# Two modes of the last weight unit loaded by SP in fp32 and cast by GpSimd, and another pace for the last jobs

## The chip, the cores and the metric

The kernel runs on one core of a Trainium2 chip. The metric is device time in microseconds of one launch. The kernel before takes 435.25 us, the median of three runs (435.19 to 435.46).

## What is computed

A causal attention with a window of 64 positions over q, k, v of 8 batches, 8 heads, 576 positions and 64 channels, and behind it a spectral mixing layer over the model width of 512:

```python
rel = pos[:, None] - pos[None, :]
mask = (rel >= 0) & (rel < 64)
attn = softmax(where(mask, q @ k.T / 8, -1e9))
x = (attn @ v)                     # laid out as (8, 576, 512)

X = np.fft.rfft(x, axis=1)         # the first 64 modes are kept
Xr, Xi = X[:, :64].real, X[:, :64].imag
Yr = einsum('bmd,mde->bme', Xr, w_r) - einsum('bmd,mde->bme', Xi, w_i)
Yi = einsum('bmd,mde->bme', Xr, w_i) + einsum('bmd,mde->bme', Xi, w_r)
y = np.fft.irfft(Y, n=576, axis=1)
u = x + y
out = u + np.maximum(u @ w_ch, 0.0)
```

w_r and w_i are 64 matrices of 512 x 512 in fp32 each, 134 MB in all, and every one is read once. The output is 9.4 MB of fp32.

## The kernel before

**Weights.** A mode is one of the 64 matrices. Four modes make a group; a group is taken in two halves hb of 256 input rows, and each half in two parts ri: 0 from w_r, 1 from w_i. One such piece, four modes of 256 rows, is a unit: 2 MB of fp32 in memory, 1 MB of bf16 in SBUF. `steps` is the order of (group, half), `wlist` the list of loads made from it, with `parts` the transfers that a load is cut into: one for the four modes in general, and for the very last load, `(len(steps) - 1, 1)`, three, of two modes, one and one.

`load_weights` issues loads on GpSimd's DMA queue (line 165), which turns fp32 into bf16 on the way. A load needs a tile of a ring. In the last phase there are only the NRA = 3 tiles of `ringA`, so a load is issued when TensorE has done its matmuls with the load three before it. `wtiles` says where a mode lies; `mode_half` (line 188) runs the matmuls of a unit. For the last unit of all it sorts them by mode, so that mode p comes first, then p + 1, p + 2, p + 3.

**Phases.** Under the loads run, one after the other: the attention; the transforms of its output; then, from the step `i == EARLY` on, the products x @ w_ch of all tiles and, under the last eight units, the jobs that bring back and multiply the modes that are complete by then. At `i == EARLY` some pools are closed (`ringB` among them) and others opened: `utpool`, from which the first output tile `utx` of [128, 2, 512] fp32 is later taken, and copies of trig tables by SP's queue (lines 951 and 952).

**Jobs.** `jobs` is a list of pairs (prepare, done). `advance` prepares the next job and finishes the one before it. When the group NGRP - 1 is complete, with eight units to go, 36 jobs are put in: eight `batch_job`s (four transposes, then four matmuls with w_ch) and, for the first four batches, seven small ones each: `early_u` (inverse transform of a tile or two) and `add_late` (one matmul, line 703, and an addition on VectorE, line 704). After each unit the loop advances until `given` has reached `want`, which grows by 36 / 6 a unit. Before the last unit but one all jobs left are finished (`half == n0 + n1 - 2`).

**The end.** After the last unit (lines 627 to 656) the last two groups are turned, multiplied and added by `early`, `full_u`, `full_z` and `last`, which write the output tile by tile, most of it from SP's queue (line 821). Output tiles come from `new_ut`: first `utx`, then the three tiles of `ringA`, two homes in each, taken round.

**Order.** The scheduling is by hand: each engine and each DMA queue runs its instructions in the order in which the program writes them; waits are added where data or memory ask for it.

Of the kernel before, what the change touches and what calls it, by code (L numbers as in the profile page):

```python
# [9 lines left out]
FP32 = mybir.dt.float32  # L10
# [16 lines left out]
def kernel(  # L27
# [10 lines left out]
    nc = tc.nc  # L38
    B, H, S, D = q.shape
    NM = moe_w_r.shape[0]  # L40
    DM = moe_w_ch.shape[0]
# [7 lines left out]
    HALF = DM // 2  # L49
    NJ = 2  # L50
# [5 lines left out]
    def pool(name, bufs=1, **kw):  # L56
        opened.append(tc.alloc_tile_pool(name=name, bufs=bufs, **kw))
        return opened[-1]

    def close(*pools):  # L60
        for x in pools:
            opened.remove(x)
            x.release()

    NLB = 4
# [33 lines left out]
    steps = [(grp, 0) for grp in range(EARLY)] + [(grp, 1) for grp in range(EARLY)]  # L99
# [4 lines left out]
    wlist = []  # L104
    for at, (grp, hb) in enumerate(steps):
        for ri in range(2):
            p = 4 * grp
            if (at, ri) == ONES:
                parts = [[(p, p + 1)], [(p + 2,)], [(p + 3,)]]
            elif (at, ri) == (len(steps) - 1, 1):  # L110
                parts = [[(p, p + 1), (p + 2,), (p + 3,)]]
            else:
                parts = [[(p, p + 1, p + 2, p + 3)]]
            wlist += [(at, part, hb, ri) for part in parts]
# [15 lines left out]
        lent.update((wstart[at] + i, t) for i, t in enumerate(of))  # L130
    lentY = Yall.rearrange("p (g j) e -> p g j e", j=NJ)
    NLY = 1
    wtiles, spent = {}, set()
    held = {"a": [], "b": [], "y": []}
    room = {"a": NRA, "b": NRB, "y": NLY}
    nload = 0
# [5 lines left out]
    def load_weights(n):  # L142
        nonlocal nload
        while nload < len(wlist):
            at, parts, hb, ri = wlist[nload]
            if 2 * n <= sum(len(ps) for ps in parts):
                return
            if nload in lent:
                w = lent[nload]
            else:  # L150
                open_to = "a" if at >= 2 * EARLY else "aby" if at < EARLY + 2 else "ab"
                h = min(open_to, key=lambda h: held[h][0] if len(held[h]) == room[h] else -1)
                if len(held[h]) == room[h]:
                    if held[h][0] not in spent:
                        return
                    held[h].pop(0)
                held[h].append(nload)
                if h == "y":
                    w = lentY
                else:  # L160
                    w = {"a": ringA, "b": ringB}[h].tile([128, 4, NJ, DM], BF16, name="wi" if ri else "wr", tag="wt")
            src = moe_w_i if ri else moe_w_r
            to = 0
            for ps in parts:
                nc.gpsimd.dma_start(  # L165
                    out=w[:, to:to + len(ps)],
                    in_=src[ps[0]:ps[-1] + 1, HALF * hb:HALF * hb + HALF, :].rearrange("g (p j) e -> p g j e", j=NJ))
                for i, p in enumerate(ps):
                    wtiles[p, hb, ri] = w[:, to + i]
                to += len(ps)  # L170
            nload += 1
            n -= to

# [21 lines left out]
    with tc.manual_schedule():  # L197
# [175 lines left out]
        at = scratch[:, 3 * NTF * NM:3 * NTF * NM + NTF]  # L373
# [104 lines left out]
        for it in range(-3, NU + 3):  # L478
# [23 lines left out]
            g = starts.get(it + 2)  # L502
# [3 lines left out]
            g = starts.get(it + 1)  # L506
# [35 lines left out]
        def bank(h, shape=(128, DM), dtype=FP32, name=None):  # L542
            return banks[h].tile(list(shape), dtype, name=name or "ps" + h, tag="bank")
# [69 lines left out]
        def advance():  # L613
            if jobs:
                prepare, done = jobs.pop(0)
                pend.append((prepare(), done))
                if len(pend) < 2:
                    return
            if pend:
                tr, done = pend.pop(0)  # L620
                done(tr)
# [108 lines left out]
        def early_jobs(b):  # L730
            early_u(b, (1,))
            add_late(b, 0)
            early_u(b, (3,))
            add_late(b, 1)
            add_late(b, 2)
            early_u(b, (0, 2))
            add_late(b, 3)
# [7 lines left out]
        NT = len(tiles)  # L745
# [6 lines left out]
        def x_jobs(pl, lo, hi):  # L752
            for i in range(lo, hi):
                def done(tr, i=i):
                    XW[i] = pl.tile([128, DM], FP32R, name=f"xw{i}")
                    nc.vector.tensor_copy(out=XW[i], in_=multiply(tr))  # L756
                jobs.append((lambda i=i: transposed(tiles[i][0]), done))
# [13 lines left out]
        ps, pu = {}, {}  # L771
# [11 lines left out]
        def tail_xw(n, js=(0, 1)):  # L783
            for i in [seq[n][j] for j in js]:
                ps[i] = bank("zt"[n % 2 == 0])
                nc.tensor.matmul(out=ps[i], lhsT=ident_r, rhs=XW[i], start=True, stop=True)  # L786
# [81 lines left out]
                nc.tensor.matmul(out=ps[i], lhsT=trigIr[:, at:at + 128], rhs=zrows(b), start=False, stop=True,  # L868
                                 skip_group_check=True)

        uts, homes = {}, []
        utpool, taken_uts = None, 0
        NUT = 2 * NRA + 1

        def new_ut():
            nonlocal taken_uts
            if not homes:
                homes.append(utpool.tile([128, 2, DM], FP32, name="utx"))
            elif taken_uts == len(homes) < NUT:
                t = ringA.tile([128, 4, DM], FP32, name="ut", tag="wt")  # L880
                homes.extend([t[:, 0:2], t[:, 2:4]])
            taken_uts += 1
            return homes[(taken_uts - 1) % NUT]
# [47 lines left out]
        NX0 = 10  # L931
        x_jobs(pool("xp0", reuse_waits="tile"), 0, NX0)
        psm = None
        half = given = 0
        n0, n1 = 2 * EARLY, 4 * (NGRP - EARLY)
        for i, (grp, hb) in enumerate(steps[EARLY:]):
            f, l = grp < EARLY or hb == 0, hb == 1
            if i == EARLY:
                while tables:
                    tables.pop(0)()  # L940
                while jobs or pend:
                    advance()
                close(stmp2, yp, ringB)
                Zall = pool("zall", side="right").tile([2 * NM, B, DM], FP32R, name="Zall")
                x_jobs(pool("xp1", side="right", reuse_waits="tile"), NX0, NT)
                utpool = pool("utpool", side="right", reuse_waits="tile")
                nc.vector.memset(YT[:, :, :, rows], 0.0)
                nc.vector.tensor_scalar(out=trz.rearrange("p c g k -> p c (g k)"), scalar1=0.0, scalar2=None, op0=ALU.mult,
                                        in0=ident.unsqueeze(1).to_broadcast([128, NDCH, 128]))
                for g in range(4):  # L950
                    nc.sync.dma_start(out=trigL[32 * g:32 * g + 16], in_=trigI[rows, 0:512])
                    nc.sync.dma_start(out=trigLr.bitcast(FP32)[32 * g:32 * g + 16], in_=trigIr.bitcast(FP32)[rows, 0:512])
                given = 0
            if f:
                psm = [bank("m"), bank("m")] if grp == LAST + 1 else bank("m")
            for ri in range(2):
                if half == n0 + n1 - 2:
                    while jobs or pend:
                        advance()
                if half == n0 + n1 - 1:  # L960
                    late["first"] = bank("z")
                    late[0][1]()
                    tail_xw(0)
                mode_half(psm, grp, hb, ri, f, l)
                load_weights(len(wlist))
                while ready:
                    ready.pop(0)()
                for t in tables[0:2]:
                    t()
                del tables[0:2]  # L970
                if half == 0:
                    nc.gpsimd.dma_start(out=wch, in_=moe_w_ch.rearrange("(c p) e -> p c e", p=128))
                if l and ri:
                    finish_group(grp, psm)
                    if grp == NGRP - 1:
                        ready.pop(0)()
                        for b in range(B):
                            batch_job(b)
                            if 0 < b <= NLB:
                                early_jobs(b - 1)  # L980
                half += 1
                if half <= n0:
                    want = max(half - 4, 0) * NX0 // (n0 - 4)
                elif half <= n0 + n1 - 8:
                    want = (half - n0) * (NT - NX0) // (n1 - 8)
                else:
                    want = NT - NX0 + (half - n0 - n1 + 8) * (B + 7 * NLB) // 6
                while given < want:
                    advance()
                    given += 1  # L990
# [74 lines left out]
```

## Time and profile before

| | |
|---|---|
| runs, median | 435.25 us |
| profiled execution, its own time | 434.85 us |
| its span, first to last instruction | 433.1 us |
| TensorE matmul, busy | 322.2 us |
| VectorE, busy | 230.0 us |
| ScalarE, busy | 179.9 us |
| GpSimd, busy | 101.3 us |
| DMA, moved | 93.64 MB, 216 GB/s over the span |
| read from HBM | 163.58 MB |
| last unit's matmuls | 395.82 to 397.01 us |

The span is what the profile sees between the first and the last instruction; 1.75 us of the execution lie around it. Bytes moved are counted as written, so a weight counts two bytes there and four in what is read from HBM. The DMA share is that of sixteen engines together; it can pass 1, since packets overlap. In a timeline each row has its start, its length, the engine, the line of the kernel, the operation, what it writes and reads, and in brackets the idle time before it with what ended it. A row of the windows has, after the stretch, its length and the busy time of TensorE's matmuls, its weight loads, VectorE, ScalarE and GpSimd with the number of instructions, then the granted clock, the DMA share and GB/s.

### The profile page before, as it was taken

How to read it: one execution, taken by the hardware profiler on the slowest of the kernel's cores; microseconds unless marked ns; L12 is line 12 of the kernel's file. 1: busy time of each engine (PE TensorE's matmuls, PEld its weight loads, DVE VectorE, ACT ScalarE, POOL GpSimd, SP SyncE). 2: the span in 40 equal slices, each digit the busy share in tenths (PEclk: the TensorE clock that was granted, in tenths of full speed). 3: DMA queues.
4: the chain of work that ended last, by engine and by line, in shares of the span. 5: the costliest groups of instructions: out<-in, count | busy, mean ns of one | idle time of the engine just before them, and what ended most of it. 6: DMA issues, size and time to landing. Idle time of an engine off the chain costs nothing.

```text
span 433.1 us, 10990 instructions
## 1 busy us (share of the span) xinstructions
PE 322.2 (74%) x4758; PEld 216.0 (50%) x4802; DVE 230.0 (53%) x472; ACT 179.9 (42%) x322; POOL 101.3 (23%) x150
## 2 busy tenths in 40 slices
PE   6888899898999999962207353767564768789994
PEld 3666667576677677641104221444343445345652
DVE  8588787876776777863104111222131315653994
ACT  5665757666666666520201100122121213325842
POOL 8322222222131231131102100012111111110990
PEclk9999999999999999996557756588899889989998
DMA  8999999999999999999999999999999999993798
GB/s 210 211 211 212 211 212 212 210 211 212 212 213 210 211 212 212 212 212 212 211 259 213 217 212 212 212 212 212 212 212 212 212 211 211 212 211 72 243 367 295
DMA packets 47280, 93.64 MB, mean 216 GB/s; under 512 B 2688, under 2 KB 3136, under 8 KB 47232
## 3 DMA queue, kind: packets, MB, share of 16 engines
q0 software_dynamic: 41008, 81.73, 99.7%
q1 hardware_dynamic: 5328, 9.77, 6.6%
q10 hardware_dynamic: 896, 1.44, 0.9%
q8 instruction: 37, 0.61, 0.5%
q14 instruction: 11, 0.09, 0.1%
HBM read 163.58 MB, written 9.44 MB: 400 GB/s over the span
## 4 chain that ended last, share of the span: by engine, by line
DMA 50%; PE 36%; issue 6%; ACT 3%; DVE 2%; POOL 1%; DVEq 0%; POOLq 0%
DMA wi<-in_moe_w_i_dram 29%; DMA wr<-in_moe_w_r_dram 22%; PE tr L231 6%; PE s L278 4%; PE s L290 3%; PE pt L298 3%; PE psm L188 3%; PE vb L243 3%; PE o L318 2%; PE s L270 2%; PE pst L786 1%; PE psz L786 1%; PE psz L610 1%; PE pst L868 1%; PE px L341 1%
## 5 line engine op out<-in xcount | busy, mean ns | idle before, releaser
L610 PE MATMUL psz<-wch,tr 128*128 128x512 f32 x176 | 62.5, 488 | 11.3 <-DMA wch<-in_moe_w_ch_dram 11.0
L756 DVE CAST xw<-psz 128x512 fp32r<-128x512 f32 x36 | 24.9, 692 | 86.1 <-PE psz L610 86.1
L584 ACT CAST tr<-ptx 128x512 fp32r<-128x512 bf16 x36 | 21.1, 586 | 102.9 <-PE ptx L603 102.9
L282 DVE TENSOR_REDUCE mx<-s 128x4 fp32r<-128x512 f32 x72 | 49.5, 688 | 26.9 <-PE s L278 26.4
L188 PEld LDWEIGHTS <-XQ 128*32 128x32 bf16 x448 | 18.9, 174 | 78.3 <-issue 53.8
L165 POOL DMA_DIRECT2D wi<-in_moe_w_i_dram x32 | 23.4, 732 | 103.6 <-PE psm L188 70.2
L188 PE MATMUL psm<-wi,XQ 128*32 128x512 bf16 x208 | 19.8, 454 | 37.1 <-DMA wi<-in_moe_w_i_dram 37.1
L610 PEld LDWEIGHTS psz<-wch,tr 128*128 128x128 f32 x176 | 37.4, 235 | 18.4 <-issue 11.6
L292 ACT ACTIVATE p<-s 128x512 bf16<-128x512 f32 x72 | 39.7, 604 | 12.8 <-PE s L290 12.8
L165 POOL DMA_DIRECT2D wr<-in_moe_w_r_dram x27 | 20.3, 754 | 95.8 <-PE psm L188 77.8
L188 PE MATMUL psm<-wr,XQ 128*32 128x512 bf16 x184 | 18.6, 483 | 28.1 <-DMA wr<-in_moe_w_r_dram 27.2
L278 PE MATMUL s<-kT,qT 64*64 64x128 bf16 (+1 forms) x576 | 29.2, 222 | 6.7 <-issue 6.7
L235 ACT COPY kT<-tr 128x576 bf16<-128x576 bf16 x32 | 23.2, 724 | 20.2 <-PE tr L231 20.2
L235 ACT COPY qT<-tr 128x576 bf16<-128x576 bf16 x32 | 23.3, 729 | 10.6 <-PE tr L231 10.6
L301 DVE COPY pts<-pt 128x1024 bf16<-128x1024 bf16 (+1 forms) x40 | 25.2, 629 | 4.5 <-PE pt L298 3.1
L278 PEld LDWEIGHTS <-qT 64*64 64x64 bf16 x576 | 17.8, 107 | 17.9 <-issue 17.5
L290 PE MATMUL s<-mx,ident_r 128*128 128x512 f32 x72 | 26.2, 437 | 0.0
L635 DVE TENSOR_TENSOR stg<-psm,Yfour 128x512 bf16<-128x512 f32 x10 | 6.9, 689 | 36.3 <-PE psm L188 36.3
L235 ACT COPY vT<-tr 128x576 bf16<-128x576 bf16 x32 | 23.3, 728 | 4.1 <-PE tr L231 4.0
L298 PE MATMUL pt<-ident_bf,p 128*128 128x128 bf16 x288 | 23.3, 221 | 1.7 <-issue 1.6
L218 POOL DMA_DIRECT2D rawk<-in_k_dram x15 | 8.1, 540 | 66.0 <-PE tr L231 59.9
L330 DVE TENSOR_TENSOR x_sb<-o,r 128x512 bf16<-128x512 f32 x32 | 22.1, 691 | 1.1
(217 smaller groups left out, 598.3 us busy)
## 6 DMA issues: line engine op xcount, KB each, us to landing
wi<-in_moe_w_i_dram POOLq DMA_DIRECT2D x29, 1024.0 KB, 18.7
wr<-in_moe_w_r_dram POOLq DMA_DIRECT2D x27, 1024.0 KB, 17.7
out_dram<-ut SPq DMA_DIRECT2D x23, 256.0 KB, 2.8
rawv<-in_v_dram POOLq DMA_DIRECT2D x16, 288.0 KB, 14.9
rawk<-in_k_dram POOLq DMA_DIRECT2D x15, 288.0 KB, 13.9
rawq<-in_q_dram POOLq DMA_DIRECT2D x15, 288.0 KB, 13.8
x_sb<-in_moe_w_r_dram POOLq DMA_DIRECT2D x2, 1024.0 KB, 15.4
out_dram<-utx SPq DMA_DIRECT2D x5, 256.0 KB, 3.1
```

What stands on the lines that cost most here:

```text
L165: nc.gpsimd.dma_start(out=w[:, to:to + len(ps)], in_=src[ps[0]:ps[-1] + 1, HALF * hb:HALF * hb + HALF, :].rearrange("g (p j) e -> p g j e" ...
L188: nc.tensor.matmul(out=ps[32 * g:32 * g + 32, 0:e], lhsT=of.rearrange("k s b m -> k (s b) m")[:, (3 * j + 1 - ri) * B:(3 * j + 5 - ri) * B ...
L231: nc.tensor.transpose(out=pt[ro, j, :], in_=raw[ro, TH * half + j, :], identity=ident_bf[ro, ro])
L235: nc.scalar.copy(out=to, in_=pt.rearrange("p j n -> p n j"))
L278: nc.tensor.matmul(out=s[ro, t, lo:128], lhsT=lq, rhs=kT[ro, 64 * n - 64 + lo:64 * n + 64], start=False, stop=True, skip_group_check=True)
L282: nc.vector.tensor_reduce(out=mx, in_=s, axis=AX.X, op=ALU.max, negate=True)
L290: nc.tensor.matmul(out=s, lhsT=ident_r, rhs=mx.unsqueeze(2).to_broadcast([128, 4, 128]), start=False, stop=True, skip_group_check=True)
L292: nc.scalar.activation(out=p[:, 4 * c2:4 * c2 + 4, :], in_=s, func=ACT_F.Exp, scale=EX_SCALE)
L298: nc.tensor.transpose(out=pt[:, t, :], in_=st[u]["p"][:, t, :], identity=ident_bf)
L301: nc.vector.tensor_copy(out=ps[:, 0:nt, :], in_=pt[:, 0:nt, :])
L610: nc.tensor.matmul(out=pz, lhsT=tr[:, c, :], rhs=wch[:, c, :], start=(c == 0), stop=(c == NDCH - 1))
L756: nc.vector.tensor_copy(out=XW[i], in_=multiply(tr))
```

## The change

In the last step, mode p of both units is no longer loaded by GpSimd's queue. SP's queue loads it in fp32 into the first output tile, 8 partitions at a time, so 16 transfers of 32 KB for a mode, and GpSimd casts it into its place in the weight tile. There is one such home: the transfers for the second unit are issued behind the cast of the first one. The cast stands in GpSimd's order behind the transfers of the same unit's other modes. The other three modes stay with GpSimd's queue: in one transfer for the unit of w_r, in two (p + 1 and p + 2, then p + 3) for that of w_i. The home `utx` is taken at `i == EARLY` and the first 16 transfers are issued there, ahead of SP's copies of the trig tables. The due count of the last jobs grows by 36 x 2 / 11 a unit in place of 36 / 6.

```diff
             elif (at, ri) == (len(steps) - 1, 1):
-                parts = [[(p, p + 1), (p + 2,), (p + 3,)]]
+                parts = [[(p,), (p + 1, p + 2), (p + 3,)]]
+            elif (at, ri) == (len(steps) - 1, 0):
+                parts = [[(p,), (p + 1, p + 2, p + 3)]]
...
+    BY_SP = list(range(len(wlist) - 2, len(wlist)))
+    homes = []
...
             for ps in parts:
-                nc.gpsimd.dma_start(
-                    out=w[:, to:to + len(ps)],
-                    in_=src[ps[0]:ps[-1] + 1, HALF * hb:HALF * hb + HALF, :].rearrange("g (p j) e -> p g j e", j=NJ))
+                if nload in BY_SP and to == 0:
+                    own = w
+                else:
+                    nc.gpsimd.dma_start(
+                        out=w[:, to:to + len(ps)],
+                        in_=src[ps[0]:ps[-1] + 1, HALF * hb:HALF * hb + HALF, :].rearrange("g (p j) e -> p g j e", j=NJ))
                 for i, p in enumerate(ps):
                     wtiles[p, hb, ri] = w[:, to + i]
                 to += len(ps)
+            if nload in BY_SP:
+                nc.gpsimd.tensor_copy(out=own[:, 0], in_=homes[0])
+                BY_SP.pop(0)
+                if BY_SP:
+                    stage_by_sp()
             nload += 1
             n -= to
+
+    def stage_by_sp():
+        at, parts, hb, ri = wlist[BY_SP[0]]
+        src = (moe_w_i if ri else moe_w_r)[parts[0][0], HALF * hb:HALF * hb + HALF, :].rearrange("(p j) e -> p j e", j=NJ)
+        for p in range(0, 128, 8):
+            nc.sync.dma_start(out=homes[0][p:p + 8], in_=src[p:p + 8])
...
-        uts, homes = {}, []
-        utpool, taken_uts = None, 0
+        uts, taken_uts = {}, 0
...
-            if not homes:
-                homes.append(utpool.tile([128, 2, DM], FP32, name="utx"))
-            elif taken_uts == len(homes) < NUT:
+            if taken_uts == len(homes) < NUT:
...
-                utpool = pool("utpool", side="right", reuse_waits="tile")
+                homes.append(pool("utpool", side="right", reuse_waits="tile").tile([128, 2, DM], FP32, name="utx"))
+                stage_by_sp()
...
-                    want = NT - NX0 + (half - n0 - n1 + 8) * (B + 7 * NLB) // 6
+                    want = NT - NX0 + (half - n0 - n1 + 8) * (B + 7 * NLB) * 2 // 11
```

## The prediction

> **What bounds the kernel now.** First the page: its totals of the engines and of the DMA queues.
>
> ```profile
> PE 322.2 (74%) x4758; PEld 216.0 (50%) x4802; DVE 230.0 (53%) x472; ACT 179.9 (42%) x322; POOL 101.3 (23%) x150
> ...
> q0 software_dynamic: 41008, 81.73, 99.7%
> ...
> q8 instruction: 37, 0.61, 0.5%
> ```
>
> q0, GpSimd's load queue, is busy in 99.7% of the engine time: up to the last weight load the DMA engines set the pace. q8 is TensorE's own code: 4758 + 4802 = 9560 instructions, and 0.61 MB / 9560 is 64 bytes each.
>
> Then the timeline of GpSimd, for the spacing of the loads:
>
> ```profile
> 372.50 0.74 POOL L165 DMA_DIRECT2D wi<-in_moe_w_i_dram  x1 [4.21 <-PE psm L188]
> 377.50 0.74 POOL L165 DMA_DIRECT2D wr<-in_moe_w_r_dram  x1 [4.26 <-PE psm L188]
> 382.46 1.81 POOL L165 DMA_DIRECT2D wi<-in_moe_w_i_dram  x3 [4.22 <-PE psp L648]
> 401.60 2.52 POOL L835 TENSOR_TENSOR utx<-x_sb,utx 128x512 f32<-128x512 f32 x2 [17.33 <-ACT utx L834]
> ```
>
> A unit of four modes every 4.98 us, so one mode is 4.98 / 4 = 1.245 us of all sixteen DMA engines. GpSimd is free between the issues, and from 384.3 to 401.6.
>
> Then one-microsecond windows over the end of the loads (the last two columns are the DMA share and GB/s):
>
> ```profile
> 389.00:390.00 1.00, 0.90 (x5) 0.29 (x3) 1.00 (x3) 0.28 (x1) 0.00 (x0) 1.00 1.11 205
> 390.00:391.00 1.00, 0.64 (x8) 0.49 (x8) 0.60 (x2) 1.00 (x3) 0.00 (x0) 1.00 0.98 182
> 391.00:392.00 1.00, 1.00 (x9) 0.73 (x6) 0.93 (x2) 0.37 (x1) 0.00 (x0) 1.00 0.68 127
> 392.00:393.00 1.00, 1.00 (x9) 0.82 (x8) 0.52 (x2) 0.82 (x2) 0.00 (x0) 1.00 0.62 117
> 393.00:394.00 1.00, 1.00 (x6) 0.65 (x5) 0.00 (x0) 1.00 (x3) 0.00 (x0) 1.00 0.57 107
> 394.00:395.00 1.00, 1.00 (x19) 0.50 (x17) 0.00 (x0) 0.69 (x2) 0.00 (x0) 1.00 0.48 90
> 395.00:396.00 1.00, 1.00 (x11) 0.57 (x11) 0.00 (x0) 0.13 (x1) 0.00 (x0) 1.00 0.19 35
> ```
>
> The share doesn't stop, it halves at about 391 and runs on to 396: about half the engines are done some 5 us ahead of the rest. Taking 1.12 as full, what is missing from 390 to 396 is 0.14 + 0.44 + 0.50 + 0.55 + 0.64 + 0.93 = 3.2, or 3.2 / 1.12 = 2.9 us of all sixteen engines. Evenly dealt, the loads would end near 393.1. The lag has a likely source: q8's 0.5% of 16 engines' span is 0.005 x 16 x 433.1 = 34.6 us of engine time, 4.3 us each if it falls on eight engines.
>
> Last the timeline of TensorE, for when it takes each load:
>
> ```profile
> 371.54 0.66 PE L188 MATMUL psm<-wr,XL 128*32 128x512 bf16 x8 [0.56 <-DMA wr<-in_moe_w_r_dram]
> 376.53 0.66 PE L188 MATMUL psm<-wi,XL 128*32 128x512 bf16 x8 [1.24 <-DMA wi<-in_moe_w_i_dram]
> 381.46 0.68 PE L188 MATMUL psm<-wr,XL 128*32 128x256 bf16 x16 [0.97 <-DMA wr<-in_moe_w_r_dram]
> 387.54 0.67 PE L188 MATMUL psm<-wi,XL 128*32 128x256 bf16 x16
> 388.14 0.88 PE L703 MATMUL psz<-Zall,trigIr 128*128 128x512 f32 x2
> 394.44 0.67 PE L188 MATMUL psm<-wr,XL 128*32 128x256 bf16 x16
> 395.82 1.19 PE L188 MATMUL psm<-wi,XL 128*32 128x256 bf16 x16
> ```
>
> Up to 381.46 it waits for loads; after that for none. The load taken at 394.44 was issued at 377.50 and, with the 13.9 us of its neighbour in the chain of waits, there by 391.4: TensorE is 3.0 us late with its jobs. Then the last unit starts at 395.82 and ends at 397.01, just behind the last landing. Both bound the end: DMA by its late half, TensorE by its jobs. From 397.4 to 426 the chain is TensorE almost without a gap, so the 36 us behind the last unit move with its end.
>
> **The change, part by part.**
>
> *Bytes.* Two modes, 0.5 MB of fp32 each, go from q0 to SP's queue. I take the same engine time per byte read: wch, fp32 into fp32, went through in the page's slice of 259 GB/s, 47 above its neighbours; 47 x 10.8 us is 0.5 MB, just its wider writes, so reading sets the rate. In all nothing is saved; it matters on which engines the SP bytes fall. Eight rows can occupy at most eight engines if a row isn't split, and no view names a packet's engine, so the price has two ends. On the early half: those engines get 2 x 2.49 us and lose 2 x 1.245 us, so they end 2.49 later (391 to 393.5), the late half 2.49 sooner (396.0 to 393.5). On the late half: 396.0 + 2.49 = 398.5. Spread over all: 0. The only rows of narrow traffic are q8's, and they show that it can sit on one half; SP's queue is another one, and the half that already carries q8 is the less likely for it. I take the early half, as a lean and not a reading.
>
> [...]
>
> *First stage.* Its 16 transfers run at about 230 to 245, are cast at 378, and their bytes are already in the sum above. In SP's queue they stand ahead of the eight copies of trigL and trigLr (229.8 to 239.4), which slip some 10 us; their reader comes at 400. Cost 0; the load queue keeps two units waiting, so no engine runs dry.
>
> *First cast.* On GpSimd behind the issue at 377.50. The issue has three modes, not four (0.7). A GpSimd copy of 128x1024 fp32 is not in the trace: above, two adds of 128x512, 2.52 us; below, its memset of 128x1024 bf16, 1.01 us. I take 1.6. Done at 377.5 + 0.7 + 1.6 = 379.8; the next issue is due at 382.46, so nothing queues behind it.
>
> *Second stage.* It starts at 379.9. Two rows of SP's timeline for an issue, and two of the list of DMA issues for a landing (last column, us):
>
> ```profile
> 238.15 0.59 SPq L951 DMA_DIRECT2D trigL<-trigI  x1
> 405.40 10.59 SPq L821 DMA_DIRECT2D out_dram<-ut  x16
> ```
>
> ```profile
> out_dram<-ut SPq DMA_DIRECT2D x23, 256.0 KB, 2.8
> ...
> trigLr<-trigIr SPq DMA_DIRECT2D x4, 32.0 KB, 4.8
> ```
>
> 0.59 to 0.66 us an issue: the sixteenth goes out at 379.9 + 15 x 0.6 = 388.9. It lands 2.8 us (queues empty) to 4.8 us (loads running) later, at 391.7 to 393.7. The second cast ends 1.0 to 2.5 us on: 392.7 to 396.2. By 4.0 and 1.6 I take 394.5. It is the last thing on GpSimd before 401.6, but the whole last unit waits for it, since that unit takes mode p first.
>
> *Jobs.* Due counts after each of the last loads: 6, 12, 18, 24, 30, 36 become 6, 13, 19, 26, 32, 36. The total is the same; the early stretches have 0.56 + 1.24 + 0.97 = 2.77 us of waiting for loads to take them in. The stretch before 394.44 loses two add_late jobs, the 0.88 at 388.14, and the one before it swaps an early_u pair and an add_late for two add_lates, some 0.5 less. Together 1.3 us (0.8 to 1.9): the matmul of 394.44 comes at 393.1.
>
> *Sum.* The last unit starts 395.82 - 394.44 = 1.38 behind that: 394.5 by TensorE, 394.5 by the cast, with the loads down by 393.5. Its 16 matmuls take 1.1: end 395.6 against 397.0, a gain of 1.4 us. Worst within this case, cast at 396.2: end 397.3, a loss of 0.3; best, TensorE 1.9 sooner and the cast no bound: 2.2. The profiled execution took 434.85 (span 433.1), which becomes 433.45; the median of the runs is 0.4 higher, 435.25, and gives 433.85.
>
> **The rivals.**
>
> *Nothing moves* (SP's bytes spread over all engines, or the second cast so late that it eats the gain): the last landing stays at 396.0 or the cast comes there. For it: no view shows engines, and the cast's margin is under 2 us. 434.9 to 435.6.
>
> *Slower by the late half.* SP's eight engines are the ones that already finish at 396. Then the last landing is 398.5, the cast hardly sooner, and the last unit ends near 399.0: +2.0 us, 437.3, up to 438. It decides as soon as more than half of SP's bytes are on late engines. For it: nothing in the trace names the engines. Against: the same as above.
>
> *Slower by narrow transfers.* Each 32 KB goes into eight rows of SBUF; if a transfer needs 1.2 us and not the 0.6 of its issue, the second stage ends at 379.9 + 19 + 2 = 401, the cast at 402.6, and the unit at 403.7: +6.7, 442. It decides from about 0.7 us a transfer (379.9 + 15 x 0.7 + 4.0 + 1.6 = 396.0, where the last unit starts now). Against: the trigL copies into 16 rows came out at their spacing of 0.6 with the loads running.
>
> [...]
>
> **How the numbers follow.** 0.61 for the forecast (433.85, own range 432.9 to 435.0), 0.14 for nothing moves, 0.19 for the late half, 0.06 for narrow transfers. A measurement of this kernel tells about 0.2%, 0.87 us, from no change. Of the first case 0.55 gain more than that and 0.06 don't; of the second a little falls on each side. Faster 0.57, same 0.17, slower 0.26. The range 432.9 to 437.3 holds the first two cases and half of the third.
>
> **What would show it.** The DMA share should fall from full to nothing within some 2 us, ending near 393.5 (right); a tail as long or longer to 398 means the late half. SP's second row of 16 issues from 379.9 to 389.5; GpSimd casts of 1.0 to 2.5 us at about 378 and 393; the matmul of 394.44 at about 393.1, the last unit ending by 395.6. I am wrong if the last unit starts at a cast later than 395, or if the DMA tail has grown.

## The result, and the profile after it

| | before | after |
|---|---|---|
| median of 4 runs, us | 435.36 (435.19 to 435.56) | 440.73 (439.47 to 443.38) |
| profiled execution, us | 434.85 | 440.06 |
| its span, us | 433.1 | 438.3 |

The ratio is 1.0135, with an interval of 1.0112 to 1.0157: 5.4 us slower, where 1.4 us faster was forecast. The time lies above the whole range.

The list of DMA queues of the kernel after (packets, MB, time of the packets as a share of sixteen engines' span):

```profile
q0 software_dynamic: 40736, 81.21, 98.3%
q1 hardware_dynamic: 5840, 10.82, 7.7%
```

and SP's queue in the kernel before:

```profile
q1 hardware_dynamic: 5328, 9.77, 6.6%
```

SP's queue moves 1.05 MB more, the two modes. Its packets took 0.077 x 438.3 = 33.7 us of all sixteen engines against 0.066 x 433.1 = 28.6: **5.2 us for two modes**, where the *Bytes* step had 2 x 1.245 = 2.5. (A share counts the packets' own times, and packets overlap: at the full share of 1.12, a microsecond of the stream counts 1.12. In this measure the plain price is 2.8.) GpSimd's queue should have lost those 2.8; it lost 0.997 x 433.1 - 0.983 x 438.3 = 1.0. Together the packets' time grew by 4.2 us instead of not at all, some 3.8 us at full share. (The shares are rounded to 0.1%, so such sums are good to some 0.4 us.)

The timeline of SP's queue after (start, length, instruction):

```profile
190.80 8.63 SPq L190 DMA_DIRECT2D utx<-in_moe_w_r_dram  x16
...
383.00 8.75 SPq L190 DMA_DIRECT2D utx<-in_moe_w_i_dram  x16
```

and GpSimd's (in brackets the idle time before, and what ended it):

```profile
208.12 0.74 POOL L172 DMA_DIRECT2D wr<-in_moe_w_r_dram  x1 [5.95 <-DMA wi<-in_moe_w_i_dram]
...
381.18 0.74 POOL L172 DMA_DIRECT2D wr<-in_moe_w_r_dram  x1 [4.23 <-PE psm L206]
381.92 1.05 POOL L179 CAST wr<-utx 128x1024 bf16<-128x1024 f32 x1
386.31 1.29 POOL L172 DMA_DIRECT2D wi<-in_moe_w_i_dram  x2 [3.34 <-PE psp L666]
396.91 1.31 POOL L179 CAST wi<-utx 128x1024 bf16<-128x1024 f32 x1 [9.31 <-DMA utx<-in_moe_w_i_dram]
```

The first of these loads has this row in the kernel before:

```profile
204.50 0.74 POOL L165 DMA_DIRECT2D wr<-in_moe_w_r_dram  x1 [4.26 <-DMA wi<-in_moe_w_i_dram]
```

The load issued at 204.50 before is issued at 208.12, right behind the first stage, and that at 377.50 at 381.18: the stream is some 3.7 us late, of which one mode loaded ahead of its turn should make only 1.2. The casts are short. The second one ends at 398.2, and that is not what the last unit waits for, as TensorE's timeline shows:

```profile
391.65 0.67 PE L206 MATMUL psm<-wi,XL 128*32 128x256 bf16 x16 [1.87 <-DMA wi<-in_moe_w_i_dram]
...
395.17 1.68 PE L628 MATMUL psz<-wch,tr 128*128 128x512 f32 x4
...
398.94 0.67 PE L206 MATMUL psm<-wr,XL 128*32 128x256 bf16 x16
...
400.33 0.68 PE L206 MATMUL psm<-wi,XL 128*32 128x256 bf16 x12
401.31 0.60 PE L206 MATMUL psm<-wi,XL 128*32 128x256 bf16 x4 [0.30 <-DMA wi<-in_moe_w_i_dram]
```

The last unit's last four matmuls wait for a load of the stream, the last landing, and end at 401.9 instead of 397.0: 4.9 us of the 5.2 by which the span grew. TensorE is only that 0.30 us ahead of the load: it had waited 1.87 us for the load taken at 391.65 and ran the jobs behind it at a lower granted clock (see the last section). Behind the last unit the tail is as before.

Windows of two microseconds over that stretch (busy time and count of TensorE, its weight loads, VectorE, ScalarE, GpSimd; then the granted clock, the DMA share and GB/s):

```profile
390.00:392.00 2.00, 0.35 (x13) 0.35 (x15) 1.35 (x3) 0.00 (x0) 0.00 (x0) 1.00 1.11 223
392.00:394.00 2.00, 1.75 (x18) 0.70 (x11) 0.00 (x0) 0.80 (x2) 0.00 (x0) 0.72 1.19 192
394.00:396.00 2.00, 2.00 (x11) 1.59 (x10) 1.00 (x2) 0.86 (x2) 0.00 (x0) 0.50 0.64 126
396.00:398.00 2.00, 2.00 (x12) 1.45 (x12) 0.45 (x2) 1.69 (x3) 1.09 (x1) 0.93 0.34 64
398.00:400.00 2.00, 2.00 (x23) 1.31 (x22) 0.00 (x0) 1.17 (x2) 0.22 (x1) 1.00 0.14 27
400.00:402.00 2.00, 1.61 (x18) 0.79 (x16) 0.16 (x1) 0.06 (x1) 0.00 (x0) 1.00 0.04 8
```

The tail of the loads has not shrunk to 393.5, it runs to 401. It is no longer one step at half height either: 0.34 of a full 1.12 is five engines of sixteen, 0.14 is two, 0.04 less than one. And at 392 to 394 the share is above full while fewer bytes move.

The trace holds one thing more that the views don't print: the landing updates. Each load of GpSimd's queue has sixteen, read here as one for each engine. For the last load they come, before, eight by 393.4 and eight from 394.7 to 396.4: the two halves that the forecast read from the share. After, fourteen come by 398.4 and two at 401.0 and 401.3.

### The profile page after: what moved, and what is told of

It reads as the page before. It is cut to its first block, busy times and chain, and to the rows that moved or that the text cites. A ratio compares the mean times of both kernels' runs of the same rounds, so it can differ in the third digit from the quotient of the medians.

```text
span 438.3 us, 11082 instructions
## 1 busy us (share of the span) xinstructions
PE 331.5 (76%) x4802; PEld 215.9 (49%) x4802; DVE 230.1 (53%) x472; ACT 180.5 (41%) x322; POOL 103.3 (24%) x151
## 4 chain that ended last, share of the span: by engine, by line
DMA 57%; PE 30%; issue 6%; DVE 3%; ACT 2%; POOL 1%; DVEq 0%; POOLq 0%
DMA wr<-in_moe_w_r_dram 33%; DMA wi<-in_moe_w_i_dram 19%; PE tr L249 5%; DMA rawk<-in_k_dram 4%; PE s L296 3%; PE s L308 3%; PE s L288 3%; PE psm L206 3%; PE pt L316 2%; PE vb L261 2%; PE o L336 2%; PE psz L804 1%; PE pst L804 1%; PE pst L886 1%; PE psm L863 1%
## 5 line engine op out<-in xcount | busy, mean ns | idle before, releaser
L288 PE MATMUL s<-mask_t,ident_bf 128*128 128x512 bf16 x72 | 28.4, 395 | 0.9 <-ACT p L310 0.8
```

The costliest lines, as they stand in the source:

```text
L288: nc.tensor.matmul(out=s, lhsT=ident_bf, rhs=mask_t[:, mk], start=True, stop=True)
```

## The experiments

Twelve kernels, each timed beside the kernel before on the same chip; losses are against the median of that one (435.19 to 435.32). The diffs are against the kernel after, unless another is named.

### The pace alone, and the change without it

The pace put into the kernel before (e1_pace_only), and the old pace put into the kernel after (e12_old_pace). The edit of the first, against the kernel before; the second is its reverse, against the kernel after:

```diff
-  want = NT - NX0 + (half - n0 - n1 + 8) * (B + 7 * NLB) // 6
+  want = NT - NX0 + (half - n0 - n1 + 8) * (B + 7 * NLB) * 2 // 11
```

> The kernel before with only the new pace of the last jobs; all weights through GpSimd's queue. If the pace is harmless (my theory), the loads end at 396 as before and the last matmul of the unit before the last comes some 1.3 us sooner than 394.4: 434.5 to 435.3. If the pace is what hurts: 438 or more.

> The changed kernel with the old pace of the last jobs (36 / 6 a unit). If the pace has no part in the loss: within 0.7 us of the change, 439.5 to 442. If the new pace is what keeps TensorE from being later still: 441.5 to 443.

Measured: e1_pace_only 435.18 us, ratio 1.0002 (0.9992 to 1.0011); e12_old_pace 439.57, ratio 1.0102 (1.0087 to 1.0117). TensorE's timeline of e1_pace_only:

```profile
386.88 0.68 PE L188 MATMUL psm<-wi,XL 128*32 128x256 bf16 x16 [0.30 <-DMA wi<-in_moe_w_i_dram]
...
393.06 0.67 PE L188 MATMUL psm<-wr,XL 128*32 128x256 bf16 x16
...
394.45 0.67 PE L188 MATMUL psm<-wi,XL 128*32 128x256 bf16 x8
...
395.61 0.60 PE L188 MATMUL psm<-wi,XL 128*32 128x256 bf16 x4 [0.50 <-DMA wi<-in_moe_w_i_dram]
396.83 0.60 PE L188 MATMUL psm<-wi,XL 128*32 128x256 bf16 x4 [0.62 <-DMA wi<-in_moe_w_i_dram]
```

The matmul of 394.44 comes at 393.06 and the last unit at 394.45 instead of 395.82; then the unit waits twice for loads, the second time until 396.83. What TensorE gained it spends waiting for the late engines: both bounds had stood at the same place, and moving one is worth nothing. The kernel after with the old pace is 1.2 us better by the medians (440.73 - 439.57), with intervals that overlap, and still loses 4.4, so the pace is not where most of the 5.4 us come from.

### How SP's rows are cut into transfers

Four kernels change only the loop of `stage_by_sp`: one transfer of all 128 rows for a mode (e2_wide), sixteen of 8 rows that lie 4 partitions apart (e3_rows_apart), eight of 16 neighbouring rows (e4_sixteen_rows), sixteen of 8 rows that lie 2 apart (e9_two_apart).

```diff
-        for p in range(0, 128, 8):
-            nc.sync.dma_start(out=homes[0][p:p + 8], in_=src[p:p + 8])
+        nc.sync.dma_start(out=homes[0], in_=src)                                          # e2
...
+        for p in range(0, 128, 32):                                                       # e3
+            for r in range(4):
+                nc.sync.dma_start(out=homes[0][p + r:p + 32:4], in_=src[p + r:p + 32:4])
...
+        for p in range(0, 128, 16):                                                       # e4
+            nc.sync.dma_start(out=homes[0][p:p + 16], in_=src[p:p + 16])
...
+        for p in range(0, 128, 16):                                                       # e9
+            for r in range(2):
+                nc.sync.dma_start(out=homes[0][p + r:p + 16:2], in_=src[p + r:p + 16:2])
```

> The changed kernel with one SP transfer of 128 rows a mode in place of 16 transfers of 8 rows. Theory 'narrow' (eight neighbouring rows make their engines spend twice the time for a byte): the 5 us are gone, 434.5 to 436. Theory 'half' (the bytes fall on half of the engines, two of them late ones): the same. Rival 'SP and fp32' (any SP transfer beside GpSimd's queue, or the wait for the cast, costs this): still 438 to 441.

> The changed kernel, still 16 transfers of 8 rows a mode on the same number of engines, but the eight rows of a transfer lie 4 partitions apart and not side by side. 'Narrow by neighbouring rows': most of the loss goes, 435 to 437. 'Half': nothing changes, 439.5 to 441.

> The changed kernel with 8 transfers of 16 neighbouring rows a mode. 'Half': sixteen engines share them, the loss goes, 434.5 to 436. 'Narrow by neighbouring rows': as many engines meet in as few rows for each, so the stream still loses about what it lost, 438 to 441.

> As the changed kernel, 16 transfers of 8 rows a mode, the rows 2 partitions apart, so they spread over 16 partitions and not 8 or 32. If crowding grows with how few rows of SBUF lie between those of a transfer: between 437 (4 apart) and 440.5 (neighbours), 437.5 to 439.5. If only direct neighbours hurt: 436.5 to 437.5.

Two more part the two ends of such a transfer: neighbours in SBUF, read from rows 4 apart (e5_near_in_sbuf), and the reverse (e6_near_in_memory). In both the rows arrive in another order than the weights', so the output is another; bytes, counts and sizes are the same.

```diff
+        for p in range(0, 128, 32):
+            for r in range(4):
+                nc.sync.dma_start(out=homes[0][p + 8 * r:p + 8 * r + 8], in_=src[p + r:p + 32:4])   # e5
...
+                nc.sync.dma_start(out=homes[0][p + r:p + 32:4], in_=src[p + 8 * r:p + 8 * r + 8])   # e6
```

> As the changed kernel, 16 transfers of 8 rows a mode, written to eight neighbouring rows of SBUF, but read from rows 4 apart in memory (so the rows of mode p of the last unit's two loads come in another order than the matmuls pair them with, and the output differs). If it is the rows of SBUF that crowd: as slow as the change, 439.5 to 441. If it is the read of one 32 KB stretch: as with rows apart, 436.5 to 437.5.

> The mirror of the run before: read from eight neighbouring rows of memory, written to rows of SBUF 4 apart (again another order of the rows of these two modes, so the output differs). If it is the rows of SBUF that crowd: 436.5 to 437.5. If it is the read: 439.5 to 441.

Measured. The last two columns are packets' time, worked out from each page's list of queues as above: what q1's packets took over the kernel before's 28.6 us, and what q0's and q1's together took over its 460.4.

| kernel | rows in SBUF | median, us | ratio | loss, us | q1, us | q0 + q1, us |
|---|---|---|---|---|---|---|
| e2_wide | all 128 | 435.97 | 1.0027 (1.0015 to 1.0040) | 0.7 | +2.7 | 0.0 |
| e3_rows_apart | 8, 4 apart | 437.11 | 1.0044 (1.0027 to 1.0061) | 1.8 | +3.2 | +0.9 |
| e9_two_apart | 8, 2 apart | 437.33 | 1.0051 (1.0035 to 1.0068) | 2.1 | +2.8 | +0.6 |
| e6_near_in_memory | 8, 4 apart | 437.59 | 1.0049 (1.0034 to 1.0064) | 2.4 | +3.2 | +0.5 |
| after | 8 neighbours | 440.73 | 1.0135 (1.0112 to 1.0157) | 5.4 | +5.2 | +4.2 |
| e5_near_in_sbuf | 8 neighbours | 440.96 | 1.0127 (1.0110 to 1.0144) | 5.7 | +5.3 | +4.2 |
| e4_sixteen_rows | 16 neighbours | 440.24 | 1.0111 (1.0096 to 1.0126) | 4.9 | +6.5 | +4.9 |

The lines behind two of the rows, q1 on the page of e5_near_in_sbuf:

```profile
q1 hardware_dynamic: 5840, 10.82, 7.7%
```

and on that of e6_near_in_memory:

```profile
q1 hardware_dynamic: 5840, 10.82, 7.3%
```

Same packets, same bytes, 0.4% of the span apart, or 2.0 us (0.077 x 439.5 - 0.073 x 435.6).

The runs fall into two groups, and what parts them is whether the 8 or 16 rows of a transfer lie side by side **in SBUF**. Neighbours in memory cost nothing that can be told (e6 beside e3), nor does the transfer's size or number by itself (e9 and the kernel after both have sixteen of 32 KB a mode), and a distance of two is enough. All 128 rows in one transfer are neighbours too, and don't pay: it is few of them that do. Two-microsecond windows over the first stage show the same from the side of the engines (last two columns: DMA share, GB/s). The kernel after:

```profile
201.00:203.00 2.00, 0.84 (x12) 0.50 (x13) 0.05 (x1) 0.59 (x1) 0.75 (x1) 0.68 1.28 182
203.00:205.00 2.00, 0.00 (x0) 0.00 (x0) 0.00 (x0) 0.00 (x0) 0.00 (x0) 0.50 1.39 174
```

e4_sixteen_rows:

```profile
197.00:199.00 2.00, 1.54 (x16) 0.51 (x12) 1.68 (x6) 0.00 (x0) 1.01 (x2) 0.65 1.29 178
199.00:201.00 2.00, 0.00 (x0) 0.00 (x0) 1.90 (x5) 0.00 (x0) 0.00 (x0) 1.00 1.43 193
```

e3_rows_apart:

```profile
201.00:203.00 2.00, 0.00 (x0) 0.00 (x0) 0.00 (x0) 0.08 (x1) 0.00 (x0) 0.50 1.12 232
203.00:205.00 2.00, 0.00 (x0) 0.00 (x0) 0.00 (x0) 0.00 (x0) 0.00 (x0) 0.50 1.13 236
```

For the first two kernels these are the densest windows. The stretch from 195 to 207 as a whole, in the kernel before, after and in e3_rows_apart:

```profile
195.00:207.00 12.00, 3.08 (x24) 1.22 (x24) 4.11 (x10) 1.86 (x3) 1.98 (x3) 0.63 1.12 212
...
195.00:207.00 12.00, 4.08 (x44) 1.48 (x37) 5.00 (x11) 0.59 (x1) 2.98 (x4) 0.64 1.21 208
...
195.00:207.00 12.00, 4.80 (x50) 1.79 (x43) 4.83 (x11) 0.59 (x1) 3.80 (x5) 0.64 1.13 231
```

With neighbours the packets' time goes up (1.28 to 1.43 in the dense windows) while the bytes go down (174 to 193); with rows apart the share stays at its 1.12, and GB/s rises over the stream's 212, since fp32 writes twice the bytes for the same read. SP's packets take longer, and so do the stream's beside them (263 ns for 172, and 193 for 173, below): q0 gives back 1.0 to 1.6 us for the two modes in these runs, 2.2 to 2.7 in the others.

The packets' own times, which the trace holds and the views only sum, show it row by row. One of SP's packets carries one row here, 4 KB. Mean time of one:

| kernel | first stage, ns | second stage, ns |
|---|---|---|
| e2_wide | 174 | 172 |
| e3_rows_apart | 172 | 171 |
| e9_two_apart | 172 | 170 |
| e6_near_in_memory | 174 | 170 |
| after | 263 | 227 |
| e5_near_in_sbuf | 258 | 253 |
| e4_sixteen_rows | 312 | 292 |

A packet of the weight stream, which reads 4 KB too, took 173 ns between 250 and 370 us; in the kernel after it took 193 between 195 and 205, beside the first stage. One other thing differs between the groups: SP issues rows that lie apart more slowly (10.87 us for the first sixteen in e3_rows_apart, 8.63 in the kernel after). That doesn't make the difference, for the packets of the first stage ran over equally long stretches, from 194.7 to 205.2 and from 194.2 to 204.4.

There is a second price: the engines no longer end as evenly. By the sums alone it can't be told, since each is good to 0.4. The tails show it. e2_wide:

```profile
394.00:396.00 2.00, 2.00 (x23) 1.26 (x21) 0.00 (x0) 1.70 (x4) 0.00 (x0) 1.00 0.49 91
396.00:398.00 2.00, 1.63 (x28) 0.85 (x19) 0.28 (x1) 0.49 (x2) 0.00 (x0) 1.00 0.05 8
```

e3_rows_apart:

```profile
394.00:396.00 2.00, 2.00 (x23) 1.23 (x21) 0.00 (x0) 1.70 (x4) 0.06 (x1) 1.00 0.24 52
396.00:398.00 2.00, 1.66 (x23) 0.96 (x16) 0.00 (x0) 0.21 (x1) 0.98 (x1) 1.00 0.13 24
```

In e2_wide 0.49 / 1.12 x 16 = 7 engines work until about 396, the kernel before's half. In e3_rows_apart it is 0.24, or 3.4 engines, and then 0.13, or 1.9, until 398. The sixteen landing updates of the last load say the same without an estimate (us):

| kernel | mean | fourteenth | last |
|---|---|---|---|
| before | 393.5 | 396.1 | 396.4 |
| e1_pace_only | 394.2 | 396.6 | 396.8 |
| e2_wide | 394.3 | 396.7 | 396.7 |
| e3_rows_apart | 394.2 | 396.7 | 398.2 |
| e9_two_apart | 394.4 | 395.7 | 398.6 |
| e6_near_in_memory | 394.2 | 396.3 | 398.7 |
| after | 396.7 | 398.4 | 401.3 |
| e5_near_in_sbuf | 396.6 | 399.0 | 401.2 |
| e4_sixteen_rows | 396.7 | 399.3 | 399.5 |

The mean tells the first price: 3.1 us with neighbours, and 0.7 to 0.9 in the others, where e1_pace_only, which moves no load, has 0.7. The distance from the mean to the last tells the second: 2.4 to 2.9 before and with transfers of 128 or 16 rows, 4.0 to 4.6 with 8. In e3_rows_apart thirteen engines have landed by 394.7, where before eight were still to come: most of the late half is done sooner, as the forecast wanted, and two or three engines are later. The reading that fits is that the eight engines with SP's bytes are some of each half. Between e2_wide and e3_rows_apart the means agree and the last comes 1.5 us later, so unevenness is what parts the two (1.1 us by the medians). In e4_sixteen_rows, the loads are down at 399.5, 3.1 us later than before; the rest of its 4.9 is TensorE, whose last unit starts at 400.94 behind jobs that ran at a granted clock of 0.50 in the window from 394 to 396.

### Half the dose

Only the mode of w_r goes by SP, the last unit's loads are as before (e11_one_mode):

```diff
-                parts = [[(p,), (p + 1, p + 2), (p + 3,)]]
+                parts = [[(p, p + 1), (p + 2,), (p + 3,)]]
...
-    BY_SP = list(range(len(wlist) - 2, len(wlist)))
+    BY_SP = [len(wlist) - 2]
```

> The changed kernel with only the mode of w_r by SP (16 transfers of 8 neighbouring rows at about 191, cast at about 381); the last load is GpSimd's in three transfers as before. If each stage of 16 costs by its crowding (stream later by some 2.6 us where 1.25 is paid back): about half of the change's loss or a little more, 437.5 to 439. If it is the second stage and its cast at the end that cost: 435 to 436.

Measured: 438.45 us, ratio 1.0062 (1.0042 to 1.0082), a loss of 3.3 us of the 5.4. SP's packets took 278 ns, and the last load's landings have their mean at 395.8 and their last at 399.0. One stage costs its share by itself; the second stage, its cast and its place near the end are not needed for it.

### Early engines only, far from the end

If the engines that finish first can be picked by cutting transfers narrower, SP's modes could still fill the gap. Both modes are staged near 240 us in space that `Zall` takes later, and cast twelve loads before the end, so that neither cast nor stage is near the tail. One mode goes in transfers of 4 rows, 8 apart (e7_four_engines_early), or of 6 rows, 21 apart (e8_six_engines_early), the other mode in one transfer; in e10_wide_early, the control, both go in one transfer each.

```diff
+        for n, (to, src) in enumerate(zip(stages, sources())):
+            if n == 0:
+                for p in range(0, 128, 32):
+                    for r in range(8):
+                        nc.sync.dma_start(out=to[p + r:p + 32:8], in_=src[p + r:p + 32:8])     # e7
...
+                for r in range(21):                                                            # e8
+                    nc.sync.dma_start(out=to[r:r + 106:21], in_=src[r:r + 106:21])
+                nc.sync.dma_start(out=to[126:128], in_=src[126:128])
...
+            else:
+                nc.sync.dma_start(out=to, in_=src)
...
+                if half == n0 + n1 - 12:
+                    cast_staged()
```

> Both modes staged by SP right after the transforms, in 8 KB that the later Zall tile takes over, cast there by GpSimd 12 loads before the end, so no wait is left at the end. The mode of w_r goes in 32 transfers of 4 rows, 8 apart, the mode of w_i in one transfer of 128 rows. A transfer of 4 rows can use four engines: each of them gets 128 KB more than its even share less 32, 3.7 us. If these four are of the early half: early end 391 + 3.7, late end 396.5 - 1.2, so the loads end at 395 and the time is 434.0 to 434.8. If one of them is late: it ends at 400, and the time is 438 to 439.

> As the run before, with the mode of w_r in 21 transfers of 6 rows, 21 apart, and one of 2 rows. If these use six engines, each gets 85 KB more less 32, 2.1 us. If all six are of the early half (the rows-apart run had two late ones among eight): the loads end at 395, 434.0 to 434.8; if the two late ones are among the six: 398.4, 436.5 to 437.5.

> Both modes by SP in one transfer of 128 rows each, right after the transforms, cast 12 loads before the end: no crowding, no uneven share, no transfer and no cast at the end, with the new pace. If SP, fp32 and the cast cost nothing by themselves: 434.8 to 435.5, as with the new pace alone. If the whole path costs: 436 or more, as the wide run (435.97) with its transfer near the end.

Measured: e7 437.00 us, ratio 1.0040 (1.0028 to 1.0052); e8 437.36, 1.0047 (1.0033 to 1.0061); e10 435.54, 1.0006 (0.9997 to 1.0016). Windows over the tail of e8_six_engines_early:

```profile
394.00:396.00 2.00, 2.00 (x12) 1.33 (x12) 0.72 (x2) 1.62 (x4) 0.00 (x0) 1.00 0.25 47
396.00:398.00 2.00, 2.00 (x23) 1.06 (x21) 0.00 (x0) 1.02 (x2) 0.00 (x0) 1.00 0.05 9
```

and its TensorE:

```profile
390.46 0.67 PE L216 MATMUL psm<-wi,XL 128*32 128x256 bf16 x16 [0.40 <-DMA wi<-in_moe_w_i_dram]
```

The same matmul in e10_wide_early:

```profile
389.50 0.68 PE L214 MATMUL psm<-wi,XL 128*32 128x256 bf16 x16 [0.39 <-DMA wi<-in_moe_w_i_dram]
```

The control is the kernel before within what can be told, so SP's queue, fp32, the casts and the extra space cost nothing by themselves. The narrow ones lose 1.5 and 1.8 us against it. Their tail is thin, in e8_six_engines_early 0.25 and 0.05 where the control still has 0.48 and 0.05: most of the late half was relieved. But TensorE takes a load at its last landing: in the kernel after, that landing is at 401.27 and the matmul that waited for it starts at 401.31. Of the last load's sixteen landings, fifteen come by 395.4 in e8_six_engines_early and by 396.2 in e7_four_engines_early, the sixteenth at 397.8 and 397.7; in the control eight come from 395.8 to 396.9. The reading that fits is that one of the few engines chosen is a late one. The matmul above, which waits for a load, comes 1.0 later than in the control, and so do the jobs behind it. With that one late engine, e7's 437.00 lies between its two ranges: it ends at 397.7 and not at 400. No record names an engine, so which one it is stays open. No kernel was found that picks early engines alone, and none of the twelve beats the kernel before.

## Why the prediction was wrong

**The step that failed is *Bytes*.** It took "the same engine time per byte read", from the load of `wch`. That is a transfer over 128 rows, and e2_wide shows that the price holds for such a one: +2.7 us for two modes against 2.8 in the same measure, and 174 and 172 ns a packet against the stream's 173. For 8 neighbouring rows it is 5.2 us, and 263 and 227 ns. The row was the nearest in type and not in shape, and the shape decided. The bounds drawn around it (all on the early half, all on the late half, spread) were bounds on *where* 2.49 us would fall; none allowed the sum itself to grow. As it grew, all sixteen landings of the last load came 3.1 us later on average, and the last of them 4.9.

**The rival "narrow transfers"** had the right cause and the wrong way to the end. It put the price on the second cast (ending at 402.6); the cast ended at 398.2, and in e3_rows_apart, with rows apart, the second cast starts at 395.94, no more than 1 us sooner. No run shows the 1.2 us a transfer in its sum: in the kernel after the sixteen transfers of the second stage finished landing 0.61 us apart ((396.80 - 387.72) / 15 by their landing updates), and those of the first 0.69 ((205.84 - 195.45) / 15). The price showed as lateness of the weight stream, from 200 us on. The row set against it, the trigL copies "at their spacing of 0.6 with the loads running", shows how fast SP issues; what 192 KB cost the stream it could not show.

What makes neighbouring rows of SBUF dear no run shows. Measured are the order of the table and its size, 5.2 / 2 = 2.6 us a mode for 8 neighbours.

**The lean to the early half** was wrong, and so was the other end: the landings fit a mix of both halves (e3_rows_apart: thirteen by 394.7, the last at 398.2). The last landing moved by 4.9 us (396.4 to 401.3): 3.1 of them are the mean of the sixteen, good to the 0.7 by which e1_pace_only's moved, and 1.8 the wider spread. In the five kernels with narrow transfers of rows that lie apart, the last landing is 0.9 to 1.9 us behind e1_pace_only's 396.8. The trace bears out eight engines, read as one for each landing update: each of SP's transfers of 8 rows has eight such updates behind a first one, where one of 4 rows has four and one of 128 rows sixteen. Which eight they are no run shows; the two late landings of e3_rows_apart speak against their being the early eight.

**Jobs** held: 394.44 became 393.06 in e1_pace_only, 1.4 sooner where 1.3 was worked out. Its worth did not: it needed the loads down by 393.5.

**The stages and casts.** The first stage starts at 190.8 and not at 230, which the sum did not use. SP issues every 0.54 us (8.63 / 16) for 0.6. The casts took 1.05 and 1.31 for 1.6. The landing of the second stage, 396.9, came 5.7 us behind the sixteenth issue (383.00 + 15 x 0.547 = 391.2), where 2.8 to 4.8 stood; nothing waited for it in the end, since the stream's own landing came at 401.3.

**Smaller slips.** q0's 99.7% is not how long the engines are busy: it sums packets that overlap, and the loads are down at 396 of 433 us. The best case within the forecast, 2.2 us, comes to 2.0 from its own terms (394.44 - 1.9 + 1.38 + 1.1 = 395.0, against 397.0). Neither changes the outcome.

**Open.** e2_wide loses 0.7 us, with an interval that excludes no loss, though its packets cost no more than the stream's; e10_wide_early loses nothing that can be told. What a wide transfer near the end costs was not parted further. Which engines carry what was not seen, nor that q8 is TensorE's code, which rests on the quotient of 64 bytes an instruction, nor that it makes one half late.

## What to carry to other kernels

In these runs a transfer's price was the time that it took from the stream, and that hung on the shape of its SBUF side: for the same bytes q1's packets took 5.2 us more with 8 neighbouring rows and 2.7 with all 128. Read such a price from the share of the queue on the page, not from its bytes. Rows two or four apart (170 to 174 ns a packet), or all 128 in one transfer (172 and 174), cost what the stream's bytes cost (173), and of these only all 128 kept the landings as even as before: the last 2.4 us behind their mean, against 4.0 to 4.5. Take a price from a row of the same shape, and give the price itself two ends, not only its place. Where two bounds end together, test each alone before adding their gains.

## What the runs showed of the hardware

- Eight or sixteen neighbouring partitions written by one transfer among a running stream: 227 to 263 ns (8) and 292 to 312 ns (16) for a 4 KB row, where rows two or four apart and all 128 take 170 to 174; packets' share up to 1.39 and 1.43 at 174 and 193 GB/s, where rows two or four apart stay at 1.13 and 231 or more over the stage.
- After a wait of TensorE late in the kernel its granted clock was halved in some runs and not in others: after the 1.87 us at 391.65 it is 0.72 and 0.50 in the next windows, and four matmuls of `wch` take 1.68 us (1.18 before). The stretch of jobs from 391.65 to 398.94 took 7.29 us; the same one in e1_pace_only, 386.88 to 393.06, 6.18. After 2.94 us in e4_sixteen_rows it fell to 0.50 too (7.32), after 1.70 in e2_wide it stayed at 1.00. Of e6_near_in_memory and e9_two_apart, which waited 1.59 and 1.55 us there, the second one alone fell to 0.50, and its stretch took 7.30 against 6.19. It need not cost time: the first one then waits for a load until 398.71, and their profiled executions took 437.43 and 437.47.
